# Four heads of scores per chain, values summed per query tile in one PSUM bank, and branch hints moved forward, in a fused attention and expert kernel

## The chip, the cores and the metric

The kernel runs on one core of a Trainium2 chip. The metric is the device time of one execution in microseconds; the number compared is the median of several runs. The engines are TensorE (PE in the profile, its weight loads PEld), VectorE (DVE), ScalarE (ACT), GpSimd (POOL) and SyncE (SP), whose queue issues nearly all transfers.

## The reference, cut to what matters

Three layers run one after the other, all in float32. Only the first is touched by most of the change; the second is where the branches are.

```python
# attention: batch 4, 8 heads, 768 positions, head size 64
scores = scale * np.matmul(q, k.transpose(0, 1, 3, 2))
keep = (pos[None, :] < 4) | ((rel >= 0) & (rel < 128))
scores = np.where(keep, scores, -1e9)
a = softmax(scores)
x = np.matmul(a, v)                      # to 3072 rows of 512
# experts: 8, each 512 -> 1024 -> 512; a row goes to one expert
e_idx = np.argmax(x @ w_gate + modality_bias[modality_id], axis=1)
out[mask] = gate_w[mask, None] * (np.maximum(x[mask] @ w1[e], 0.0) @ w2[e])
# last layer: 512 -> 2048 -> 512 on all rows
h = x @ w_in
out = (h / (1 + np.exp(-1.702 * h))) @ w_out
```

## The kernel before, in words

**Attention** (`attention`, lines 41 to 415) goes through 24 query tiles of 128 rows, six for each of four sequences. A tile sees its own 128 keys, the 128 before them and four sink keys, so a head's scores are 128 x 260 (128 x 128 in the first tile of a sequence). Heads are worked in four couples c, two heads a per couple. For each tile: q and k are transposed (`qtrans`, `ktrans`, lines 152 and 163) and copied out (`qevac`, `kevac`); `scores` (line 182) multiplies one couple, the two heads on the two halves of the array's rows; `mask` (196, VectorE) adds the mask and finds the extreme; `expo` (205, ScalarE) takes the exponential; `ptrans` (217) transposes the probabilities of a couple; `pevac` (240) copies them to SBUF, even couples on ScalarE, odd ones on VectorE; `pv` (270) multiplies by the values; `oevac` (288, ScalarE) copies the sums out; `back` (293) transposes them back and adds the sinks' part; `norm` (313, VectorE) divides and SP stores the rows; `logits`, `then` and `pick` choose the expert of each row. A tile's sinks go through `sinksplit`, `sinktrans` and `sinkevac`.

A float32 product is issued as two passes, and two heads of a couple use halves of the array, so that their passes run side by side. The probabilities lie in `pts` so that one product of a value tile with 256 columns serves two query tiles: those keys as "own" keys of one and as "previous" keys of the next. The sums of two neighbouring query tiles therefore lie side by side in each of two PSUM banks `ops`, one bank per four heads; they are cleared by ScalarE (`zero`, line 266) and every product adds to them.

PSUM has eight banks: three for the small tiles of tag "t" (transposes, `back`; line 55, `NT_BUFS` in 442), two for `ops`, three for scores (line 96, `NS_BUFS` in 441).

The order of all this is written out by numbers: `AT` (line 30) gives each kind of step a due time, in units of one couple (four to a tile), `kinds` (352) says how many couples one call covers, and lines 355 to 415 sort all calls by time and emit them. Each engine then works through its instructions in that order. `OPEN` (37) and `MORE` (38) give the due times of the start of the expert layer, which is mixed into the end of attention: the first expert with 256 rows among the first 16 tiles is found, its weights are loaded and split (`split`, line 1198), its first rows are gathered and transposed (`x0`, `x1`), and its first products (`first0`, `first1`) are issued, while the last tiles are still on their way.

**Experts** (`layers`, line 1103). Rows are handled in pairs of 128-row slots (`pair`, 1407) and then in lone slots (`one`, 1505), an expert's weights in eight chunks f. How many pairs and lone slots there are is known at run time only. So the pairs from the ninth on and all lone slots stand in nested `tc.If`, whose condition is a register loaded from `sx` by `counts` (1444); the body of each is followed in the code by that of the next, and leaving is a branch to the `Else` far behind. Ahead of each such branch stands a hint (`hint`, 1288): a value of 0 or 1 is loaded from rows 7 and 8 of `sx` on all five engines, and a hint instruction with this register says whether the branch will be taken. It stands at chunk f == 6 of the pair or lone slot. Within the lone slots, loads of the next weights stand in an `If` for all engines (1496).

**Last layer**: `up` and `down` over six groups of 512 rows, twice.

Of the kernel before, what the change touches and what calls it, by code (L numbers as in the profile page):

```python
# [21 lines left out]
E = 8  # L22
# [7 lines left out]
AT = dict(sinkevac=13.229, oevac=13.14, qevac=-3.201, kevac=-0.864, scores=-0.497, mask0=0.153, mask1=0.329, expo0=0.53, ptrans=2.608, pevac=3.3,  # L30
          expo1=1.235, pv=6.555, qtrans=-4.329, ktrans=-1.83, back=14.129, sinktrans=12.315, norm=14.975, logits=18.7, then=19.826, pick=23.746,
          guard=7.159, invert=12.135, zero=5.2, sinksplit=8.053)
PVU = 2
# [3 lines left out]
OPEN = dict(split1=2.989, x0=5.244, split0=4.299, x1=5.358, split2=5.494, split3=6.448, first0=6.769, first1=7.711, split4=14.718)  # L37
MORE = 85.058, 0.617, 92.724, 1.445


def attention(tc, cst, late, first, spare, q, k, v, wg, xd, then, pick, at_tile, more, opening):
# [8 lines left out]
    with ExitStack() as ctx:  # L50
# [33 lines left out]
        NV, NG = 6, 3  # L84
        zs = per.tile([P, 1], F32, name="zs")
        nc.gpsimd.memset(zs, 0.0)


        pts = per.tile([P, NG, 4, 2, 2, P], F32, name="pts")
        ops = [ps_o.tile([P, 2, 2, P], F32, name=f"ops{i}") for i in range(2)]  # L90
# [91 lines left out]
        def scores(t, c):  # L182
# [3 lines left out]
            for a in range(2):  # L186
# [26 lines left out]
        def where(t, kk):  # L213

            return kk if t % NG else 1 - kk

        def ptrans(t, c):
            i = t % NT
            ps = ps_t.tile([P, 2, 2, P], F32, name=f"pt{t}_{c}", tag="t")
            k0, k1 = where(t, 0), where(t, 1)  # L220
            for a in range(2):
                h = 2 * c + a
                if i > 0:
                    nc.tensor.transpose(ps[:, k0, a, :], pn[t][:, h, 0:P], ident)
                    nc.tensor.transpose(ps[:, k1, a, :], pn[t][:, h, KB : KB + P], ident)
                else:
                    nc.tensor.transpose(ps[:, k1, a, :], pn[t][:, h, 0:P], ident)
            tps[("p", t, c)] = ps

        def pview(t, c, x):  # L230
            if t % NT == 0:
                return x[:, t % NG, c, :, t % 2, :]
            a, b = sorted(((t - 1) % NG, t % NG))
            return x[:, a : b + 1 : b - a, c, :, t % 2, :]

        def psrc(t, c):
            ps = tps[("p", t, c)]
            return ps[:, where(t, 1)] if t % NT == 0 else ps
# [103 lines left out]
        def fill(n):  # L342
            for _ in range(n):
                nc.tensor.matmul(ops[1].rearrange("p c i t -> p (c i t)")[:, 0:256], cst["nothing"][:, 0:P], cst["nothing"], start=True, stop=True)
# [3 lines left out]
        def ok(t):  # L348
# [3 lines left out]
        kinds = dict(sinkevac=(4, sinkevac), oevac=(2, oevac), qevac=(4, qevac), kevac=(4, kevac), scores=(1, scores), mask0=(1, lambda t, c: mask(t, 2 * c)),  # L352
                     mask1=(1, lambda t, c: mask(t, 2 * c + 1)), expo0=(1, lambda t, c: expo(t, 2 * c)), expo1=(1, lambda t, c: expo(t, 2 * c + 1)),
                     ptrans=(1, ptrans), pevac=(1, pevac), pv=(PVU, pv), qtrans=(4, qtrans), ktrans=(4, ktrans), back=(2, back), sinktrans=(4, sinktrans), norm=(2, norm), logits=(4, logits), then=(4, lambda t: then(t, lgs.pop(t))), pick=(4, pick), guard=(4, guard), invert=(4, invert), zero=(2, zero), sinksplit=(4, sinksplit))
# [3 lines left out]
        for g in range(2):  # L358
            todo.append((len(F2) + .001, zero, (0, g)))
        for nm, (size, fn) in kinds.items():  # L360
            for n in range(0, 4 * T, size):
                t, c = divmod(n, 4)
                if nm in ("qtrans", "qevac", "ktrans", "kevac", "zero") and t == 0 or nm.startswith("sink") and t % NT < 2:
# [1281 lines left out]
```

## Time and profile before

| what | value |
|---|---|
| runs | 1102.95, 1104.8, 1104.44 us; median 1104.44 |
| profiled execution | 1102.95 us, span 1101.4 us from the first to the last instruction |
| TensorE busy | 1068.0 us, 97% of the span, 6625 products |
| VectorE, ScalarE, GpSimd busy | 553.7, 418.2, 241.9 us |
| mean granted TensorE clock | 0.989 of full speed |

The profile is one execution. Times in its rows are microseconds from the start of the span. L194 is line 194 of the kernel before. In timelines, rows of one kind that follow each other are joined (x4), with the start of the first; a note in brackets gives the idle time of the engine just before the row and what ended it. The duration of a product runs to its modelled end; products overlap, so what one costs is read from start to start.

### The profile page before, as it was taken

To read this page: it belongs to the slowest core of one execution; us is meant where nothing else is said; L and a number is where in the kernel's file an instruction comes from. 1 tells how busy PE (TensorE), PEld (TensorE's weight loads), DVE (VectorE), ACT (ScalarE), POOL (GpSimd) and SP (SyncE) were. 2 spreads that over 40 slices of the span, in tenths; PEclk is the share of its full clock that TensorE was granted. 3 is DMA by queue.
4 is the path that set the end of the run, shared out by engine and by line. 5 is a ranking of instruction groups with operands and counts; after the bars stand their busy time and mean duration, and the time that the engine had idled before them with its cause. 6 is when DMAs were issued, how large, how long until landed. Compare 5 with 4: busy or idle time off the path is not lost. (4 is left out here: it accounts for less than half of the span.)

```text
span 1101.4 us, 18806 instructions
## 1 busy us (share of the span) xinstructions
PE 1068.0 (97%) x6625; PEld 904.5 (82%) x6625; DVE 553.7 (50%) x1385; ACT 418.2 (38%) x1026; POOL 241.9 (22%) x397
## 2 busy tenths in 40 slices
PE   6999999978999999999989999999999999999996
PEld 4676767668999999999978888888888888888885
DVE  3767767886555665522114665655623424334232
ACT  3887778742223332222222332332323222222221
POOL 2532231253243342211001213222200101001011
PEclk8999999998999999999999999999999999999998
DMA  6555565451445532216561322302203303124011
GB/s 122 127 125 126 112 138 118 103 146 60 136 123 161 181 98 79 79 52 197 172 217 55 115 83 73 113 8 70 77 1 115 91 24 116 32 83 153 1 39 39
DMA packets 172115, 108.91 MB, mean 99 GB/s; under 512 B 118000, under 2 KB 149744, under 8 KB 171984
## 3 DMA queue, kind: packets, MB, share of 16 engines
q1 hardware_dynamic: 167184, 91.62, 30.1%
q0 software_dynamic: 4800, 15.73, 4.3%
q8 instruction: 60, 0.98, 0.4%
q14 instruction: 71, 0.58, 0.2%
HBM read 79.85 MB, written 27.48 MB: 97 GB/s over the span
## 5 line engine op out<-in xcount | busy, mean ns | idle before, releaser
L1170 PE MATMUL pu<-xh,wah 128*128 128x256 f32 (+1 forms) x576 | 185.6, 322 | 0.0
L1170 PE MATMUL pu<-xh,wal 128*128 128x256 f32 (+1 forms) x576 | 184.2, 320 | 0.4 <-DVEq L1279 0.4
L1555 DVE TENSOR_TENSOR raw<-pu,raw 128x512 f32<-128x512 f32 x96 | 66.3, 691 | 235.2 <-ACT raw L1554 232.7
L1170 PE MATMUL pu<-xl,wah 128*128 128x256 f32 (+1 forms) x576 | 184.2, 320 | 0.1
L1554 ACT ACTIVATE raw<-pu 128x512 f32<-128x512 f32 x96 | 57.5, 598 | 291.9 <-PE pu L1170 291.2
L1185 PE MATMUL pa<-h,wah 128*128 128x256 f32 x768 | 155.4, 286 | 0.0
L1185 PEld LDWEIGHTS pa<-h,wah 128*128 128x128 f32 x768 | 128.0, 194 | 0.0
L1170 PEld LDWEIGHTS pu<-xh,wal 128*128 128x128 f32 x576 | 110.4, 192 | 8.2 <-DVEq L1279 0.6
L1170 PEld LDWEIGHTS pu<-xh,wah 128*128 128x128 f32 x576 | 110.5, 192 | 7.8 <-ACTq L1279 0.2
L1170 PEld LDWEIGHTS pu<-xl,wah 128*128 128x128 f32 x576 | 110.3, 192 | 7.8 <-DVE xl L1123 0.3
L1185 PE MATMUL pa<-h,wal 128*128 128x256 f32 x384 | 109.6, 285 | 0.0
L1193 ACT ACTIVATE h<-pu 128x256 fp32r<-128x256 f32 x96 | 36.8, 383 | 184.2 <-PE pu L1170 182.6
L202 DVE CUSTOM_DVE_ANT_0 sc<-s,m 128x260 f32<-128x260 f32 (+1 forms) x192 | 73.0, 399 | 51.9 <-PE s L194 46.9
L1196 DVE SCALAR_TENSOR_TENSOR h<-pu,h 128x256 fp32r<-128x256 f32 x96 | 40.3, 422 | 110.8 <-ACT h L1193 61.7
L211 ACT ACTIVATE pn<-sc,mx 128x260 f32<-128x260 f32 (+1 forms) x192 | 92.0, 482 | 5.4 <-DVE mx L202 4.7
L1122 ACT ACTIVATE h<-raw 128x512 fp32r<-128x512 f32 x96 | 60.7, 633 | 77.7 <-DVE raw L1555 77.7
L1177 PE MATMUL pa<-wah,h 128*128 128x512 f32 x216 | 76.4, 390 | 0.0
L1177 PE MATMUL pa<-wbh,h 128*128 128x512 f32 x216 | 76.3, 389 | 0.0
L1170 PE MATMUL pu<-xh,wbh 128*128 128x512 f32 x192 | 74.8, 390 | 1.2 <-ACT y L1493 1.2
L1170 PE MATMUL pu<-xh,wbl 128*128 128x512 f32 x192 | 74.7, 389 | 0.0
L1170 PE MATMUL pu<-xl,wbh 128*128 128x512 f32 x192 | 74.7, 389 | 0.0
L1185 PEld LDWEIGHTS pa<-h,wal 128*128 128x128 f32 x384 | 74.6, 194 | 0.0
(327 smaller groups left out, 2055.8 us busy)
## 6 DMA issues: line engine op xcount, KB each, us to landing
raw<-in_moe_w_dram SPq DMA_DIRECT2D x64, 256.0 KB
cd<-yb SPq DMA_DIRECT2D x20, 512.0 KB
xd<-xe SPq DMA_DIRECT2D x24, 256.0 KB
raw<-yp SPq DMA_DIRECT2D x12, 512.0 KB
qn<-in_q_dram SPq DMA_DIRECT2D x22, 256.0 KB
kn<-in_k_dram SPq DMA_DIRECT2D x22, 256.0 KB
vn<-in_v_dram SPq DMA_DIRECT2D x22, 256.0 KB
yb<-y SPq DMA_DIRECT2D x10, 512.0 KB
```

The lines of the kernel that those rows point to most:

```text
L202: nc.vector.tensor_tensor_reduce(out=sc[:, :n], in0=ps[:, :n], in1=m[:, :n], scale=1.0, scalar=3.0e38, op0=ALU.add, op1=ALU.min, accum_out=mx)
L211: nc.scalar.activation(out=pn[t][:, h, :n], in_=sc[:, :n], func=AF.Exp, scale=-1.0, bias=mx, accum_out=sums[t][:, h : h + 1])
L1122: A.activation(out=hi, in_=x, func=AF.Copy)
L1170: nc.tensor.matmul(ps[:, 0:n], w[a][:, s], cols(x, b, k), start=(k == 0 and i == 0), stop=(k == 3 and i == 2))
L1177: nc.tensor.matmul(acc, h[a][:, s], w[b][:, 512:], start=(f == 0 and j == 0), stop=(f == last and j == 2))
L1185: nc.tensor.matmul(acc[:, i % 2 * 256 : i % 2 * 256 + 256], wa[f][a][:, s], h[b], start=(f == 0 and i % 2 == 0 and j == 0), stop=(f == CH ...
L1193: A.activation(out=hi, in_=ps, func=AF.Relu)
L1196: V.scalar_tensor_tensor(out=lo, in0=ps, scalar=0.0, in1=hi.bitcast(F32), op0=ALU.max, op1=ALU.subtract)
L1554: A.activation(out=s, in_=ps, func=AF.Sigmoid, scale=1.702)
L1555: V.tensor_tensor(out=s, in0=ps, in1=s, op=ALU.mult)
```

## The change

In attention, `scores` takes two couples per call (four heads, four banks), `ops` is one bank with 128 columns per couple, `pv` sums a query tile's own and previous keys by itself with 128-column products, so that clearing (`zero`) and the arrangement of `pts` by three key tiles go, and nearly all due times are new. In the expert layer a hint is static ("LikelyTaken") and stands in an `If` that holds only when the exit will be taken; it stands at f == 3 (5 in the last unconditional pair) and, for lone slots, f == 2. Rows 7 and 8 of `sx` go. The `If` around the loads of lone slots runs on SP alone.

```diff
-AT = dict(sinkevac=13.229, oevac=13.14, qevac=-3.201, kevac=-0.864, scores=-0.497, mask0=0.153, mask1=0.329, expo0=0.53, ptrans=2.608, pevac=3.3,
-          expo1=1.235, pv=6.555, qtrans=-4.329, ktrans=-1.83, back=14.129, sinktrans=12.315, norm=14.975, logits=18.7, then=19.826, pick=23.746,
-          guard=7.159, invert=12.135, zero=5.2, sinksplit=8.053)
-PVU = 2
+AT = dict(sinkevac=10.229, oevac=10.224, qevac=-2.123, kevac=-1.366, scores=-0.449, mask0=-0.2, mask1=0.21, expo0=0.692, ptrans=2.608, pevac=3.437,
+          expo1=0.867, pv=7.004, qtrans=-4.358, ktrans=-1.915, back=10.991, sinktrans=9.575, norm=11.395, logits=15.779, then=16.626, pick=20.835,
+          guard=5.52, invert=11.081, sinksplit=8.614)
...
-OPEN = dict(split1=2.989, x0=5.244, split0=4.299, x1=5.358, split2=5.494, split3=6.448, first0=6.769, first1=7.711, split4=14.718)
-MORE = 85.058, 0.617, 92.724, 1.445
+OPEN = dict(split1=4.183, x0=5.146, split0=3.966, x1=5.358, split2=5.428, split3=6.826, first0=6.763, first1=6.923, split4=14.582)
+MORE = 84.738, 0.617, 92.724, 1.62
...
-        pts = per.tile([P, NG, 4, 2, 2, P], F32, name="pts")
-        ops = [ps_o.tile([P, 2, 2, P], F32, name=f"ops{i}") for i in range(2)]
+        ops = ps_o.tile([P, 4, P], F32, name="ops")
+        pts = {}
...
-        def scores(t, c):
+        def scores(t, g):
...
-            for a in range(2):
+            for c, a in ((2 * g, 0), (2 * g, 1), (2 * g + 1, 0), (2 * g + 1, 1)):
...
         def pevac(t, c):
+            if c == 0:
+                pts[t] = p2.tile([P, 4, 2, 2, P], F32, name=f"pts{t}", tag="pts")
+            k = slice(1, 2) if t % NT == 0 else slice(0, 2)
+            x, ps = pts[t][:, c, k], tps.pop(("p", t, c))[:, k]
             if c % 2:
-                nc.vector.tensor_copy(pview(t, c, pts), psrc(t, c))
+                nc.vector.tensor_copy(x, ps)
             else:
-                nc.scalar.activation(out=pview(t, c, pts), in_=psrc(t, c), func=AF.Copy)
+                nc.scalar.activation(out=x, in_=ps, func=AF.Copy)
...
-        def zero(t, g):
-
-            nc.scalar.activation(out=ops[g][:, :, t % 2, :], in_=zs.unsqueeze(2).broadcast_to([P, 2, P]), func=AF.Copy)
-
-        def pv(t, g=None):
+        def pv(t, g):
 
             i = t % NT
-            if i == 0:
-                return
-            kw = dict(start=False, stop=False, skip_group_check=True)
-            for j in [t - 1] + ([t] if i == NT - 1 else []):
-                for h in range(H) if g is None else range(4 * g, 4 * g + 4):
-
-                    c, a = divmod(h, 2)
-                    o = ops[c // 2][64 * a : 64 * a + 64, c % 2]
-                    if j == t - 1:
-                        nc.tensor.matmul(o.rearrange("p i t -> p (i t)"), nat[j]["v"][:, h], pts[:, j % NG, c, a].rearrange("p i t -> p (i t)"), **kw)
-                    else:
-                        nc.tensor.matmul(o[:, t % 2, :], nat[j]["v"][:, h], pts[:, j % NG, c, a, t % 2, :], **kw)
+            for c in (2 * g, 2 * g + 1):
+                for kk in range(i == 0, 2):
+                    for a in range(2):
+                        nc.tensor.matmul(ops[64 * a : 64 * a + 64, c], nat[t - 1 + kk]["v"][:, 2 * c + a], pts[t][:, c, kk, a], start=(kk == 0 or i == 0), stop=(kk == 1), skip_group_check=True)
...
-            nc.scalar.activation(out=ohl[t][:, 2 * g : 2 * g + 2], in_=ops[g][:, :, t % 2, :], func=AF.Copy)
+            nc.scalar.activation(out=ohl[t][:, 2 * g : 2 * g + 2], in_=ops[:, 2 * g : 2 * g + 2], func=AF.Copy)
...
-NS_BUFS = 3
+NS_BUFS = 4
...
-    def hint(label, row, i):
-
-        v = nc.values_load(sx[0:1, row, i : i + 1], engines=ENGINES, min_val=0, max_val=1)
-        tc.mark_branch_hint_location(label, v, engines=ENGINES)
+    def hint(label, n, i):
+
+        with tc.If(n <= i):
+            tc.mark_branch_hint_location(label, "LikelyTaken", engines=ENGINES)
...
-            if f == 5 and u == NP0 - 1:
+            if f == 3 and u == NP0 - 1:
                 counts()
-            if f == 6 and NP0 - 1 <= u < NP - 1:
-                hint(f"pairs{u + 1}", 7, u + 1)
+            if f == (5 if u == NP0 - 1 else 3) and NP0 - 1 <= u < NP - 1:
+                hint(f"pairs{u + 1}", pairs[0], u + 1)
...
         alone.append(nc.values_load(sx[0:1, 2, E + 1 : E + 2], min_val=0, max_val=E))
+        alone.append(flag(2, E + 1, (ET.SP,)))
...
-            with tc.If(alone[0] > s + 1):
+            with tc.If(alone[1] > s + 1):
...
-            if f == 6 and s + 1 < E:
-                hint(f"alone{s + 1}", 8, s + 1)
+            if f == 2 and s + 1 < E:
+                hint(f"alone{s + 1}", alone[0], s + 1)
```

## Rows read from the trace of the kernel before

**Rows 1.** Table by stage: stretch, length, busy time (instructions) by engine, PE clock, DMA share, GB/s.
```profile
67.80:119.50 51.70, 51.70 (x390) 35.35 (x388) 35.43 (x152) 41.32 (x143) 13.24 (x45) 1.00 0.57 123
...
213.00:240.80 27.80, 20.70 (x180) 17.03 (x179) 21.60 (x53) 16.38 (x36) 16.30 (x22) 1.00 0.64 184
```

**Rows 2.** Timeline of PE around a change of sequence: start, duration, what, count.
```profile
110.48 0.71 PE L194 MATMUL s<-kts,qt 64*128 64x260 f32 x4
111.12 1.08 PE L282 MATMUL ops<-pts,vn 128*64 128x256 f32 x8
112.13 0.33 PE L224 MATMUL pt<-ident,pn 128*128 128x128 f32 x1
112.30 0.27 PE L225 MATMUL pt<-ident,pn 128*128 128x128 f32 x1
112.41 0.27 PE L224 MATMUL pt<-ident,pn 128*128 128x128 f32 x1
112.52 0.27 PE L225 MATMUL pt<-ident,pn 128*128 128x128 f32 x1
112.72 0.49 PE L194 MATMUL s<-kts,qt 64*128 64x128 f32 x4
113.14 0.33 PE L224 MATMUL pt<-ident,pn 128*128 128x128 f32 x1
...
113.53 0.27 PE L225 MATMUL pt<-ident,pn 128*128 128x128 f32 x1
...
119.37 1.08 PE L282 MATMUL ops<-pts,vn 128*64 128x256 f32 x8
120.28 0.61 PE L284 MATMUL ops<-pts,vn 128*64 128x128 f32 x8
120.82 0.44 PE L227 MATMUL pt<-ident,pn 128*128 128x128 f32 x2
```

**Rows 3.** Timeline of DVE: the copy of the transposes that ended at 113.53.
```profile
113.84 0.69 DVE L242 COPY pts<-pt 128x512 f32<-128x512 f32 x1 [0.19 <-PE pt L225]
```

**Rows 4.** Timeline of PE on the way out of attention.
```profile
226.12 0.98 PE L1134 MATMUL pu<-ident,xg 128*128 128x128 f32 x7 [1.63 <-ACT xg L1143]
...
233.14 0.37 PE L298 MATMUL bt<-svb,stt 96*128 96x288 f32 x1 [1.47 <-DVE xe L319]
```

**Rows 5.** Timeline of DVE on the way out of attention.
```profile
232.56 0.44 DVE L319 TENSOR_TENSOR xe<-bt,rs 128x288 f32<-128x288 f32 x1
...
234.92 2.35 DVE L675 CUSTOM_DVE_ANT_0 pk_d<-lg,bias 128x8 f32<-128x8 f32 x1 [0.29 <-POOL lg L330]
...
237.88 1.99 DVE L678 SCALAR_TENSOR_TENSOR pk_eq<-pk_d,pk_mx,c_rank 128x8 f32<-128x8 f32 x1
```

**Rows 6.** Groups by line from 20 to 220 us: busy, mean ns, idle before.
```profile
L268 ACT ACTIVATE ops<-zs 128x256 f32<-128x256 f32 x47 | 18.1, 386 | 1.4
```

**Rows 7.** Timeline of POOL on the way out of attention.
```profile
234.85 2.41 POOL L1123 TENSOR_TENSOR wal<-raw,wah 128x1024 fp32r<-128x1024 f32 x1
```

**Rows 8.** Timeline of PE where the lone experts are left.
```profile
563.12 2.02 PE L1491 MATMUL pa<-ca,raw 128*128 128x128 f32 x16 [1.69 <-SPq L1496]
566.37 0.47 PE L1170 MATMUL pu<-xh,wbh 128*128 128x512 f32 x1 [1.23 <-ACT y L1493]
```

**Rows 9.** Hints and branches of PE's queue: ns least/median/most, first and last start.
```profile
L1641 PEldq BRANCH_PREFETCH_HINT x1: 35/35/35, 557.9 to 557.9; - x1
L1528 PEldq COMPARE_BRANCH x1: 3003/3003/3003, 560.0 to 560.0; - x1
L1496 PEldq COMPARE_BRANCH x3: 223/500/2503, 559.3 to 563.7; - x3
L1641 PEldq BRANCH_PREFETCH_HINT x1: 55/55/55, 1.0 to 1.0; - x1
L1072 PEldq COMPARE_BRANCH x1: 494/494/494, 6.8 to 6.8; - x1
```

**Rows 10.** Waits from 526 to 534 us: total, times, longest.
```profile
PE pu L1482 <- DVEq L1384: 0.8, 1, 0.8
```

More of the change, by code (lines that the diff above doesn't have):

```diff
@@ L83, in attention @@
         m0, m1, m2 = cst["m0"], cst["m1"], cst["m2"]
-        NV, NG = 6, 3
-        zs = per.tile([P, 1], F32, name="zs")
-        nc.gpsimd.memset(zs, 0.0)
-        pts = per.tile([P, NG, 4, 2, 2, P], F32, name="pts")
-        ops = [ps_o.tile([P, 2, 2, P], F32, name=f"ops{i}") for i in range(2)]
+        NV = 6
+        ops = ps_o.tile([P, 4, P], F32, name="ops")
+        pts = {}
         sctx = ctx.enter_context(ExitStack())
@@ L211, in expo @@
             nc.scalar.activation(out=pn[t][:, h, :n], in_=sc[:, :n], func=AF.Exp, scale=-1.0, bias=mx, accum_out=sums[t][:, h : h + 1])
-        def where(t, kk):
-            return kk if t % NG else 1 - kk
         def ptrans(t, c):
@@ L219, in ptrans @@
             ps = ps_t.tile([P, 2, 2, P], F32, name=f"pt{t}_{c}", tag="t")
-            k0, k1 = where(t, 0), where(t, 1)
             for a in range(2):
@@ L223, in ptrans @@
                 if i > 0:
-                    nc.tensor.transpose(ps[:, k0, a, :], pn[t][:, h, 0:P], ident)
-                    nc.tensor.transpose(ps[:, k1, a, :], pn[t][:, h, KB : KB + P], ident)
+                    nc.tensor.transpose(ps[:, 0, a, :], pn[t][:, h, 0:P], ident)
+                    nc.tensor.transpose(ps[:, 1, a, :], pn[t][:, h, KB : KB + P], ident)
                 else:
-                    nc.tensor.transpose(ps[:, k1, a, :], pn[t][:, h, 0:P], ident)
+                    nc.tensor.transpose(ps[:, 1, a, :], pn[t][:, h, 0:P], ident)
             tps[("p", t, c)] = ps
[L230 to L238, printed above, removed]
         def pevac(t, c):
+            if c == 0:
+                pts[t] = p2.tile([P, 4, 2, 2, P], F32, name=f"pts{t}", tag="pts")
+            k = slice(1, 2) if t % NT == 0 else slice(0, 2)
+            x, ps = pts[t][:, c, k], tps.pop(("p", t, c))[:, k]
             if c % 2:
-                nc.vector.tensor_copy(pview(t, c, pts), psrc(t, c))
+                nc.vector.tensor_copy(x, ps)
             else:
-                nc.scalar.activation(out=pview(t, c, pts), in_=psrc(t, c), func=AF.Copy)
+                nc.scalar.activation(out=x, in_=ps, func=AF.Copy)
         stt, sts = {}, {}
@@ L343, in fill @@
             for _ in range(n):
-                nc.tensor.matmul(ops[1].rearrange("p c i t -> p (c i t)")[:, 0:256], cst["nothing"][:, 0:P], cst["nothing"], start=True, stop=True)
+                nc.tensor.matmul(ops.rearrange("p c t -> p (c t)")[:, 0:256], cst["nothing"][:, 0:P], cst["nothing"], start=True, stop=True)
         fill(F1)
@@ L349, in ok @@
             return 0 <= t < T
-        kinds = dict(sinkevac=(4, sinkevac), oevac=(2, oevac), qevac=(4, qevac), kevac=(4, kevac), scores=(1, scores), mask0=(1, lambda t, c: mask(t, 2 * c)),
+        kinds = dict(sinkevac=(4, sinkevac), oevac=(2, oevac), qevac=(4, qevac), kevac=(4, kevac), scores=(2, scores), mask0=(1, lambda t, c: mask(t, 2 * c)),
                      mask1=(1, lambda t, c: mask(t, 2 * c + 1)), expo0=(1, lambda t, c: expo(t, 2 * c)), expo1=(1, lambda t, c: expo(t, 2 * c + 1)),
-                     ptrans=(1, ptrans), pevac=(1, pevac), pv=(PVU, pv), qtrans=(4, qtrans), ktrans=(4, ktrans), back=(2, back), sinktrans=(4, sinktrans), norm=(2, norm), logits=(4, logits), then=(4, lambda t: then(t, lgs.pop(t))), pick=(4, pick), guard=(4, guard), invert=(4, invert), zero=(2, zero), sinksplit=(4, sinksplit))
+                     ptrans=(1, ptrans), pevac=(1, pevac), pv=(2, pv), qtrans=(4, qtrans), ktrans=(4, ktrans), back=(2, back), sinktrans=(4, sinktrans), norm=(2, norm), logits=(4, logits), then=(4, lambda t: then(t, lgs.pop(t))), pick=(4, pick), guard=(4, guard), invert=(4, invert), sinksplit=(4, sinksplit))
         todo = []
@@ L357, in attention @@
             todo.append((n + AT["scores"] + .001, fill, (some,)))
-        for g in range(2):
-            todo.append((len(F2) + .001, zero, (0, g)))
         for nm, (size, fn) in kinds.items():
@@ L362, in attention @@
                 t, c = divmod(n, 4)
-                if nm in ("qtrans", "qevac", "ktrans", "kevac", "zero") and t == 0 or nm.startswith("sink") and t % NT < 2:
+                if nm in ("qtrans", "qevac", "ktrans", "kevac") and t == 0 or nm.startswith("sink") and t % NT < 2:
                     continue
@@ L410, in attention @@
         todo.append((last("scores", "mask0", "mask1"), close, (sctx, "scores")))
-        todo.append((last("pv", "zero", "expo0", "expo1"), close, (tctx, "values")))
+        todo.append((last("pv", "expo0", "expo1"), close, (tctx, "values")))
         for nm, time in OPEN.items():
@@ L952, in steps @@
     def steps():
-        sx = pool.tile([P, 9, NQ], I32, name="sx")
+        sx = pool.tile([P, 7, NQ], I32, name="sx")
         V.memset(sx, 0)
@@ L981, in steps @@
             V.tensor_tensor(out=sx[:, r], in0=y, in1=new, op=ALU.mult)
-            if r == 1:
-                V.tensor_copy(sx[:, 7], y)
-        V.tensor_scalar(out=sx[:, 8, 0:E], in0=cst["col"][:, 0:E], scalar1=e1[:, E : E + 1], scalar2=None, op0=ALU.is_lt)
         V.tensor_scalar(out=sx[:, 2, E : E + 1], in0=e2[:, E : E + 1], scalar1=0.5 / P, scalar2=1.0, op0=ALU.mult, op1=ALU.add)
```

## Prediction

> **What bounds the kernel now.** I read the table by stage first. In the attention stage TensorE is busy in 51.70 of 51.70 us at full clock, with ScalarE at 41.32 and VectorE at 35.43 [rows 1]. A busy share alone does not show that TensorE sets the pace, so the second view is its timeline there: chain follows chain with the same lengths every time, 0.64 us for two heads of scores, 1.01 us for four heads of values [rows 2]. An engine that waited for others would show varying gaps. So a tile costs what its chains cost, and the reader is to see that a chain costs more than its columns: something is paid whenever the kind of work changes. The third view is the way from attention into the experts, 213 to 240.8 us, where TensorE is busy for 20.70 of 27.80 us [rows 1], and the fourth the leaving of the lone experts, where it stands still twice (below). The steps between (pairs of experts, 267.6 to 533.5 us) and the last layer run without a gap, and no edit touches their work.
>
> **Scores and values, the prices.** All from [rows 2], start to start. Inside a run of transposes one takes 0.11 (112.41 to 112.52). The first after values takes 0.17 (112.13 to 112.30), the last before scores 0.20 (112.52 to 112.72): such a run pays 0.06 + 0.09 = 0.15 for being entered and left. A chain of two heads of scores takes 0.64 with 260 keys (110.48 to 111.12) and 0.42 with 128 (112.72 to 113.14). It has four passes in two side-by-side pairs, so 2 x 132 columns cost 0.22, 2 x 260 columns 0.43, and the remaining 0.21 is paid per chain. Eight passes of values with 256 columns take 1.01 (111.12 to 112.13); eight with 256 and eight with 128 take 1.45 (119.37 to 120.82). So eight with 128 cost 0.44, eight with 256 twice that, and a chain of values pays about 0.15 on top.
>
> **What the change makes of it.** Per tile there are two chains of scores for four, two runs of transposes and the like for four, and still two chains of values, which now hold 16 passes of 128 columns for 8 of 256: 0.88 + 0.15 = 1.03 for 1.01. That is 2 x 0.21 + 2 x 0.15 - 2 x 0.02 = 0.68 us less per tile. The first tile of each of the four sequences has no values today and gets two chains: 0.30 of overhead, so it saves 0.38 (its own columns, 2 x 0.44, are those that the last tile of the sequence gives up). 20 x 0.68 + 4 x 0.38 = **15.1 us less**.
>
> **What it adds there.** The three small PSUM banks are taken in turn by transposes, q or k, transposes, and then `back`, which now stands last in the run and needs the bank of the first transposes. Its copy by VectorE is over 1.00 us after the last of these began (113.53 to 113.84 + 0.69) [rows 2, 3]; TensorE has 9 x 0.11 = 0.99 us to do until `back`. TensorE went on 0.14 us after a VectorE operation that freed a bank had ended (232.56 + 0.44 to 233.14) [rows 4, 5]. So `back` is about 0.15 late, in two runs of each of 20 tiles (those of first tiles copy half as much): 40 x 0.15 = **6.0 us more**. Behind the waiting `back` stand values and scores, so all of it counts. Ends: 0 if another bank is free, 0.35 each (14 us) if VectorE is one more row late.
>
> **What costs nothing while its cover holds.** The cleared accumulators go: 47 ScalarE activations, 18.1 us [rows 6], on an engine that was not the limit. Four score banks for three: the next chain needs its first bank half a tile later, some 4 us, and VectorE has 35.43 / 12 = 3.0 us of work in each half of the six tiles of that stage [rows 1]. If that cover goes, each half tile stretches by what is missing. The probabilities keep two buffers of a tile, read long before the next but one. SP issues the same loads in the same order; the first expert's weights come later in its order by up to 1.2 of the planner's steps, behind the stores of tile rows that come earlier, and the first use of the late ones is after routing begins. The loads of hint values from memory go on five engines; a compare on each comes in their place, in stretches where TensorE runs without gaps and its sequencer is ahead.
>
> **The way out of attention.** In the new order `back` of tile 22 is ahead of the first expert's transposes and that of tile 23 behind all else. The 1.47 us stop before it, for a VectorE operation that stood behind other work [rows 4], goes: **1.5 less**, or nothing if ScalarE's copy of the values is late instead. The 1.63 us stop for the gathered rows [rows 4] stays, as the value chains between lookup and use are as many. After the last `back`, two VectorE operations of 8 columns took 2.35 and 1.99 us [rows 5], the first for the length of a GpSimd split that began just before it (234.85, 2.41 us) [rows 7]. The last choice of experts is ordered ahead of one split now: I take half of one, **1.2 less**, between 0 and 4.3.
>
> **The hints.** On TensorE the hint for leaving the lone experts ran at 557.9, the branch at 560.0 took 3.00 us, and TensorE stood still for 1.69 us [rows 8, 9]. A jump without any hint, at 563.7, took 2.50 [rows 9]: 2.1 us of notice bought nothing. With notice of 5.8 us (1.0 to 6.8), at the start of the program, a branch over a long body took 0.49 [rows 9]. The change moves the hint from the seventh to the third of eight chunks; a chunk is two groups of eight passes of 0.11 us, so that is 7 us more. I side with the long notice: **1.7 less**, between 0 and 2.9, as the second stop of 1.23 [rows 8] follows the unhinted jump. At the exit of the pairs TensorE waited 0.8 us for VectorE [rows 10], which had the last sums to copy, not for code: nothing there. The Trainium skill, "Runtime: NRT & Kernel Launch", section "Instruction fetch mechanics", says that fetching ahead is purely sequential and that a taken branch to code outside the window forces a fetch before anything goes on. By that the hint would buy nothing at any distance; the first two rows agree, the third does not.
>
> **The sum.** -15.1 + 6.0 - 1.5 - 1.2 - 1.7 = -13.5 us. The profiled execution took 1102.95 (span 1101.4), so 1089.4; the median of the runs shown is 1.5 above it, so **1090.9** for the median. What a measurement of this kernel can tell from no change is about 0.2%, 2.2 us.
>
> **Rivals.**
> *Hints do nothing.* For it: 3.00 us with a hint, 2.50 without. Against: 0.49. It gives 1092.6.
> *The waits for banks are at their upper end.* For it: `back` has no slack in the new order. Against: VectorE is idle for three tenths of the stage [rows 1], so it is seldom a row late. 14 for 6: 1099.
> *Slower: the one accumulator bank is a gate.* Today each group of four heads has its bank, with two halves, and a copy-out has most of a tile of time. After the change each chain of values must wait for ScalarE's copy-out of the same heads of the tile before, twice per tile. If ScalarE gets to it late by x, TensorE stands for x in each of 48 chains; from 13.5 / 48 = 0.28 us on, the change loses, and at 0.45 the time is 1112. Against: the copy is as large as a clearing, under 0.4 [rows 6], there are some 3 us between two chains of values, and ScalarE, busy for 0.8 of the stage [rows 1], loses the 18.1 us of clearing. [...]
> *The new value passes don't run side by side.* Then 16 passes cost 16 x 0.11 and a chain 0.88 more: 1130. Against: eight passes of 128 columns take 0.44 today in the same alternation of halves.
>
> **How the numbers follow.** Forecast with working hints 0.57, with idle ones 0.24, upper bank waits 0.08, gate 0.06, no pairing 0.02, no change by other causes 0.03. The first three are faster but for 0.02 of the bank case that could end near zero: faster 0.88, same 0.05, slower 0.07. Low end: no bank waits (-6.0) and some of the 3.1 us of split and the 1.2 us of the second stop, 1082. High end: half of the added bank waits and idle hints, with the small terms gone, 1098.
>
> **What would show it.** Right: four-head chains of scores of 1.07 us, chains of values of 1.03, two of each per tile; a tile 0.5 us shorter; no L268 rows; idle time before `back` put down to VectorE's or ScalarE's copies; the lone experts' exit branch under 0.5 us and no stop before the first L1491 row behind it. Wrong: chains of values that begin late after ScalarE's copy-out; gaps inside a chain of scores; a tile as long as today; a stop at the exit as long as today.

## The result, and the profile after

| | before | after |
|---|---|---|
| median of four runs each | 1104.62 us | 1093.67 us (1092.24 to 1094.46) |
| ratio, 95% interval | | 0.9899, 0.988 to 0.9918 |
| profiled execution, span | 1102.95, 1101.4 us | 1093.89, 1092.3 us |
| TensorE busy, products | 1068.0 us, 6625 | 1059.9 us, 6945 |
| ScalarE busy | 418.2 us | 406.1 us |

The change is 11 us faster. The forecast was 1090.9 within 1082 to 1098: direction and range hold, and the time came out 2.8 us above the forecast by the median and 4.5 us above it in the profiled execution (1093.89 against 1089.4). Line numbers below are those of each kernel; L191 after is L194 before, and so on.

The table by stage, the stretch that answers to the first of [rows 1] and the way out of attention (stretch, length, busy time by engine in the order PE, PEld, DVE, ACT, POOL, PE clock, DMA share, GB/s):

```profile
66.67:116.45 49.78, 49.64 (x470) 39.80 (x470) 35.27 (x152) 38.59 (x130) 13.19 (x45) 1.00 0.58 129
205.30:233.70 28.40, 22.05 (x213) 18.48 (x210) 22.05 (x55) 16.08 (x36) 17.35 (x25) 1.00 0.63 180
```

Six tiles take some 1.9 us less in these windows, 0.32 a tile, 80 more products included. ScalarE's 41.32 has become 38.59, but TensorE, still without a real gap, sets the pace. The way out of attention is no shorter.

The timeline of PE in the new order, one half tile, which answers to [rows 2]:

```profile
92.40 1.15 PE L191 MATMUL s<-kts,qt 64*128 64x260 f32 x8
93.47 0.33 PE L216 MATMUL pt<-ident,pn 128*128 128x128 f32 x1
...
93.86 0.27 PE L217 MATMUL pt<-ident,pn 128*128 128x128 f32 x1
93.97 0.60 PE L153 MATMUL qp<-ident,qn 128*128 128x128 f32 x4
...
94.73 0.27 PE L217 MATMUL pt<-ident,pn 128*128 128x128 f32 x1
95.01 0.73 PE L275 MATMUL bt<-btw,oh 128*128 128x144 f32 x4
95.67 1.09 PE L258 MATMUL ops<-pts,vn 128*64 128x128 f32 x16
96.69 1.15 PE L191 MATMUL s<-kts,qt 64*128 64x260 f32 x8
```

The timeline of DVE, the copy that `back` waits for, which answers to [rows 3], and that of ACT, the copies of the summed values out of their bank:

```profile
94.17 0.69 DVE L228 COPY pts<-pt 128x512 f32<-128x512 f32 x1
```

```profile
92.55 0.36 ACT L265 ACTIVATE oh<-ops 128x256 f32<-128x256 f32 x1
...
97.00 0.38 ACT L265 ACTIVATE oh<-ops 128x256 f32<-128x256 f32 x1
```

Four heads of scores take 1.07 (92.40 to 93.47), a chain of values 1.02 (95.67 to 96.69). The last transpose before `back` is followed after 0.28 us and not 0.11: the copy of the first transposes ends at 94.86, `back` starts 0.15 later, at 95.01.

The timeline of PE on the way out, which answers to [rows 4], with the first product of routing:

```profile
218.63 0.33 PE L1102 MATMUL pu<-ident,xg 128*128 128x128 f32 x1
220.38 0.98 PE L1102 MATMUL pu<-ident,xg 128*128 128x128 f32 x7 [1.42 <-ACT xg L1111]
...
225.06 0.29 PE L272 MATMUL bt<-svb,stt 96*128 96x288 f32 x1
...
233.74 0.24 PE L797 MATMUL pt<-pk_oh,c_ones 128*128 128x192 bf16 x1 [4.14 <-DVE pk_oh L644]
```

The timelines of DVE and of POOL there, which answer to [rows 5] and [rows 7]:

```profile
224.24 0.42 DVE L1164 SCALAR_TENSOR_TENSOR h<-pu,h 128x256 fp32r<-128x256 f32 x1 [1.00 <-ACT h L1161]
...
227.09 0.46 DVE L293 TENSOR_TENSOR xe<-bt,rs 128x288 f32<-128x288 f32 x1
227.47 2.18 DVE L647 CUSTOM_DVE_ANT_0 pk_d<-lg,bias 128x8 f32<-128x8 f32 x1
...
229.58 2.39 DVE L650 SCALAR_TENSOR_TENSOR pk_eq<-pk_d,pk_mx,c_rank 128x8 f32<-128x8 f32 x1
231.89 0.45 DVE L293 TENSOR_TENSOR xe<-bt,rs 128x288 f32<-128x288 f32 x1
...
232.67 0.17 DVE L647 CUSTOM_DVE_ANT_0 pk_d<-lg,bias 128x8 f32<-128x8 f32 x1
```

```profile
223.07 2.41 POOL L1091 TENSOR_TENSOR wal<-raw,wah 128x1024 fp32r<-128x1024 f32 x1 [3.27 <-ACT wah L1090]
...
227.22 4.73 POOL L1091 TENSOR_TENSOR wal<-raw,wah 128x1024 fp32r<-128x1024 f32 x2
```

The stop before the `back` of tile 23 is gone, that for the gathered rows is there. Two operations of 8 columns are stretched again, 2.18 and 2.39 us, and the second ends with the second of the two GpSimd splits (229.58 + 2.39 = 231.97, 227.22 + 4.73 = 231.95); the same operation as the first takes 0.17 once the splits are over.

The timeline of PE where the lone experts are left, which answers to [rows 8], and the hints and branches of PE's queue (least, median, most, in ns), which answer to [rows 9]:

```profile
553.61 2.84 PE L1460 MATMUL pa<-ca,raw 128*128 128x128 f32 x24
557.39 0.47 PE L1138 MATMUL pu<-xh,wbh 128*128 128x512 f32 x1 [0.94 <-ACT y L1462]
```

```profile
L1610 PEldq BRANCH_PREFETCH_HINT  x2: 40/42/45, 509.5 to 542.9; - x2
L1497 PEldq COMPARE_BRANCH  x2: 358/1170/1982, 552.5 to 554.3; - x2
```

The hint for the lone exit runs at 542.9, 9.6 us ahead of the exit branch at 552.5, which takes 0.36 us where it took 3.00 before; the first stop is gone. The jump behind it at 554.3, which has no hint, takes 1.98, and the stop of TensorE after it is still there.

### The profile page after: what moved, and what is told of

The parts are those of the page before. It is cut to its first block, busy times and chain, and to the rows that moved or that the text cites. A ratio compares the mean times of both kernels' runs of the same rounds, so it can differ in the third digit from the quotient of the medians.

```text
span 1092.3 us, 19270 instructions
## 1 busy us (share of the span) xinstructions
PE 1059.9 (97%) x6945; PEld 920.8 (84%) x6945; DVE 552.9 (51%) x1383; ACT 406.1 (37%) x978; POOL 241.5 (22%) x396
## 4 chain that ended last, share of the span: by engine, by line
PE 47%; issue 4%; POOL 0%; ACT 0%; POOLq 0%; DVE 0%; ACTq 0%
PE pu L1138 22%; PE pa L1145 17%; PE pu L1145 6%; PE pu L1451 1%; PE pa L1460 1%; POOL out_dram L1548 0%; POOLq L1610 0%; DVE raw L1524 0%; PE pt L1102 0%; ACT xs L1121 0%; ACT raw L1523 0%; ACT y L1462 0%; ACT ca L1453 0%; POOLq L1548 0%; ACTq L1462 0%
```

## The experiments

"From the first scores" below is the span of the profiled execution less the start of the first scores, which came at 15.5 to 17.6 us in the fourteen profiles, whatever the kernel. It is 1084.4 before and 1075.7 after. "The lone stretch" is from the first product of the lone experts to the first of the last layer: 32.84 before, 30.59 after.

### The hints without the new order

The new hints in the kernel before, with all that comes with them: their places, the counts read earlier, the `If` on SP alone, and rows 7 and 8 of `sx` gone. Attention stays as it was.

```diff
...
-            if f == 6 and s + 1 < E:
-                hint(f"alone{s + 1}", 8, s + 1)
+            if f == 2 and s + 1 < E:
+                hint(f"alone{s + 1}", alone[0], s + 1)
...
```

> The kernel before with the new hints alone; attention is that of before. My theory: early static hints are worth the stop at the exit of the lone experts and part of the one behind it, 1.7 to 2.3 us of 1104, so 1102.4; on TensorE the exit branch takes under 0.5 us (3.00 before), no stop before the first L1491 row behind it, and the pairs' exit keeps its 1.12 us gap. Rival 'hints do nothing, the traces differ by chance': branch 2.5 to 3 us, time 1104.5. Rival 'the loads of hint values on five engines cost time too': more than 2.5 us less, and a shorter stretch from the first unconditional pair to the last pair.

Measured: 1100.98 beside 1104.16, ratio 0.9967 (0.9957 to 0.9978). The stop in the middle of the lone exit is gone and the lone stretch takes 30.43 us. The exit branch, the jump behind it, and TensorE's first product of the last layer:

```profile
L1526 PEldq COMPARE_BRANCH  x2: 192/762/1332, 558.9 to 560.7; - x2
```

```profile
563.62 0.47 PE L1167 MATMUL pu<-xh,wbh 128*128 128x512 f32 x1 [0.78 <-issue]
```

The branch itself took 1.33, not under 0.5: the time came out better than expected, the duration of the branch worse. The jump took 0.19 here, and TensorE still stood for 0.78, so the second stop is for the most part not the jump's. The rival that hints do nothing falls. The sign of the third one, that the loads of hint values cost time too, did come: more than 2.5 us less. But `early_register` below keeps these loads and gains as much, and from routing's first product to the lone experts it is as long as before (292.71 for 292.70).

### The new order without the hints

The changed kernel with the hints of before (the edit above, reversed).

> The changed kernel with the hints of before (register, chunk 6). My theory: the two halves add up, so 1093.7 + 2.2 = 1095.9, 0.992 of before; attention, tail and routing as in the changed kernel (routing at full rate by 261.7 us, 268.4 before); the exit branch of the lone experts is at 3 us again and the stop of 1.7 is back. Rival 'the hints were worth nothing and the exit got shorter because of where the code lies now': 1093.7, exit branch under 0.5 us.

Measured: 1095.28, ratio 0.9918 (0.9903 to 0.9934). The lone stretch is 31.45, the exit branch (least, median, most, in ns):

```profile
L1499 PEldq COMPARE_BRANCH  x1: 2121/2121/2121, 553.2 to 553.2; - x1
```

Routing was where the changed kernel has it (its first product at 233.77). The ratios multiply to 0.9918 x 0.9967 = 0.9885, which lies within the interval of the whole. So the order brings about 9 us and the hints the rest: by the medians 3.2 us in the old order, and in the new one 1.6 beside the first median of the changed kernel (1093.67) and 1.0 beside its second (1094.33, below), which is hard to tell from none.

### Notice or form of the hint

The kernel before with its register hints moved forward, and the changed kernel with its static hints moved back:

```diff
...
-            if f == 6 and s + 1 < E:
+            if f == 2 and s + 1 < E:
                 hint(f"alone{s + 1}", 8, s + 1)
```

> The kernel before with its register hints at the new, earlier chunks (3 and 5 for pairs, 2 for lone slots). Theory 'notice is what counts': exit branch of the lone experts under 0.5 us, 1.7 to 2.3 us less than before. Rival 'the static form is what counts': branch 2.5 to 3 us, time as before, 0.998 to 1.002.

Measured: 1101.13, ratio 0.9973 (0.9963 to 0.9983), 3 us less than before; the lone stretch is 30.62.

```diff
...
-            if f == 2 and s + 1 < E:
+            if f == 6 and s + 1 < E:
                 hint(f"alone{s + 1}", alone[0], s + 1)
```

> The changed kernel with its static hints at the old place, chunk 6. Theory 'notice is what counts': the exit branch of the lone experts takes 2 to 3 us with some 2 us of notice, the stop behind it is back, 1.7 to 2.3 us more than the changed kernel: 1095.9. Rival 'the static form is what counts': branch under 0.5 us, 1093.7.

Measured: 1094.41, ratio 0.991 (0.9892 to 0.9928); the lone stretch is 31.54. The rows of the exit branch, first with the early register (the most of three branches is the exit), then with the late static hint (the exit and the jump behind it):

```profile
L1528 PEldq COMPARE_BRANCH  x3: 65/65/456, 531.8 to 560.4; - x3
```

```profile
L1497 PEldq COMPARE_BRANCH  x2: 2109/2673/3237, 551.3 to 553.7; - x2
```

With a register 10 us ahead the branch takes 0.46. With the static form 1.6 us ahead it takes 2.11, and the jump behind it 3.24. **Notice counts, the form does not**, by the duration of the branch and the lone stretch. The price is smaller than expected in the new order: the time is 0.7 above the first median of the changed kernel and 0.1 above its second, too little to tell from none, and the lone stretch is 0.95 longer. All eleven profiles with the early place (most of them below) have a lone stretch of 30.4 to 30.7, the three with the late one 31.4 to 32.8.

### Two heads per chain of scores again

```diff
-kinds = dict(... scores=(2, scores) ...
+kinds = dict(... scores=(1, scores) ...
...
-        def scores(t, g):
+        def scores(t, c):
...
-            for c, a in ((2 * g, 0), (2 * g, 1), (2 * g + 1, 0), (2 * g + 1, 1)):
+            for a in range(2):
```

> The changed kernel with scores of one couple per call again, so two heads per chain; due times, the four score banks and the summing of values are those of the changed kernel, and by the due times every second chain of scores falls between the two runs of transposes. My theory, prices per chain and per run: 48 chains more, each 0.21 of its own and 0.15 for the run that it cuts, 17.3 us; it gives 0.64 us of other work between the transposes and the back-transposition, so the wait of 6.9 us goes; 1093.7 + 17.3 - 6.9 = 1104, a tile 0.4 us longer. Rival 'the gain is from the values and the clearing, not from the chains of scores': 1092 to 1096.

Measured: 1101.03, ratio 0.9974 (0.9963 to 0.9986), 7.4 us above the changed kernel, 8.6 from the first scores. The timeline of PE:

```profile
93.16 0.27 PE L217 MATMUL pt<-ident,pn 128*128 128x128 f32 x1
93.26 0.66 PE L275 MATMUL bt<-btw,oh 128*128 128x144 f32 x4
93.85 1.09 PE L258 MATMUL ops<-pts,vn 128*64 128x128 f32 x16
94.87 0.71 PE L191 MATMUL s<-kts,qt 64*128 64x260 f32 x4
95.51 0.33 PE L216 MATMUL pt<-ident,pn 128*128 128x128 f32 x1
```

`back` follows the transposes after 0.10: the wait is gone, as expected, 0.7 us in all for 6.9. Put back, 48 chains cost (8.6 + 6.2) / 48 = 0.31 each, where 0.36 was expected. The rival that the gain is from the values and the clearing, 1092 to 1096, falls. With 1101.03 this kernel, which has the new hints, the new value chains, the new due times and no clearing, is where the kernel before with the new hints alone is (1100.98). So the four-head chains carry the gain of the order, and what else the order brings, the 18.1 us less of ScalarE's clearing included, comes to nothing on balance. No run takes these other parts one by one.

### `back` behind the values

```diff
-AT = dict(... back=10.991, ...
+AT = dict(... back=11.04, ...
```

> The changed kernel with one due time moved: back 10.991 to 11.04, so that it follows the chain of values instead of the transposes. Theory 'the 0.15 before it is a wait for the bank, until VectorE's copy ends': the wait goes, and two more changes of the kind of work come instead, by the rows 0.20 + 0.31 + 0.22 for 0.11 + 0.15 + 0.22 + 0.20 per half tile; 0.05 x 45 = 2 us more, 1093.7 to 1097, and the first product of back starts at the same distance each time. Rival 'it is the price of going from transposes to back': then 0.2 x 45 = 9 us more, 1103.

Measured: 1094.82, ratio 0.9912 (0.9896 to 0.9929), from the first scores 1075.9. The timeline of PE:

```profile
95.33 0.27 PE L217 MATMUL pt<-ident,pn 128*128 128x128 f32 x1
95.53 1.09 PE L258 MATMUL ops<-pts,vn 128*64 128x128 f32 x16
96.55 0.76 PE L275 MATMUL bt<-btw,oh 128*128 128x144 f32 x4
97.24 1.15 PE L191 MATMUL s<-kts,qt 64*128 64x260 f32 x8
```

The rival is out: 1103 was its price. No such wait is left, and a half tile (92.99 to 97.24) takes 4.25 against 4.29, six tiles 49.75 against 49.77, so the new changes of work cost what the wait had. `two_chains` too has `back` straight behind the transposes and does not wait, so it is a real wait and not the price of going from the one to the other; with this order of work it is not worth moving.

### The way out of attention

```diff
-OPEN = dict(... split2=5.428, ...
+OPEN = dict(... split2=5.05, ...
```

> The changed kernel with the third weight split due before the transposes of the gathered rows instead of behind them (split2 5.428 to 5.05). ScalarE can do its half in the 1.4 us in which it waits for these rows, and GpSimd then starts its row of splits some 3 us sooner. My theory, VectorE's operations of 8 columns are held until GpSimd's split ends: one of the two blocked ones (2.18 and 2.39 us) goes, the product behind the last choice starts at 231.5 (233.74 in the changed kernel), 1091.5. Rival 'the tail goes by something else, a blocked operation is cover only': 1093.7, product at 233.5 or later.

Measured: 1093.32, ratio 0.9903 (0.9887 to 0.992): no gain. My theory's arrangement missed its aim: the first split did start sooner, but ScalarE's halves of the next two still waited for the first expert's products, GpSimd was splitting at 229.52 and 232.19, and two operations were held for 2.05 and 1.75 us. That tells nothing of the theory.

```diff
-OPEN = dict(split1=4.183, x0=5.146, split0=3.966, x1=5.358, split2=5.428, split3=6.826, first0=6.763, first1=6.923, split4=14.582)
+OPEN = dict(split1=4.183, x0=16.9, split0=3.966, x1=16.905, split2=16.91, split3=16.93, first0=16.92, first1=16.94, split4=16.95)
```

> The changed kernel with the first expert's transposes, its third to fifth weight splits and its first products due behind the last choice of experts (x0 16.9, x1 16.905, split2 16.91, first0 16.92, split3 16.93, first1 16.94, split4 16.95), so the last tile's back-transpositions are ahead of them on TensorE and no split runs on GpSimd beside the last choice. My theory, the way from the last tile to routing sets the time and the blocked operations cost 4 us of it: no operation of 8 columns over 0.4 us, the choice done by 223, TensorE busy with the first expert until some 228 and the routing's first product then, 5 us sooner; 1088 to 1090. Rival 'the splits and copies moved behind the choice collide with the routing on VectorE and GpSimd': routing as much later as it began sooner, 1092 to 1095.

Measured: 1092.13, ratio 0.9892 (0.9876 to 0.9909), just inside the rival's range; from the first scores it is 2.5 less, half of the gain that my theory expected, and operations were held all the same. The choice was done at 224.4, 9 us sooner, but routing's first product had to stand behind the first expert's (230.63), and the splits now met the routing. The timelines of DVE and POOL:

```profile
230.15 1.70 DVE L772 TENSOR_TENSOR pk_d<-pk_d,pk_mx 128x64 f32<-128x64 f32 x1
...
232.36 1.80 DVE L821 TENSOR_TENSOR r_n<-r_cx 128x8 f32<-128x8 f32 x1
...
234.59 2.08 DVE L777 TENSOR_SCALAR g_sm<-g_sm 128x8 f32<-128x8 f32 x1
```

```profile
229.37 4.76 POOL L1091 TENSOR_TENSOR wal<-raw,wah 128x1024 fp32r<-128x1024 f32 x2 [1.70 <-ACT wah L1090]
...
234.25 2.40 POOL L1091 TENSOR_TENSOR wal<-raw,wah 128x1024 fp32r<-128x1024 f32 x1
```

Each ends with a GpSimd split, and two more of 2.08 (234.59) and 1.65 (237.58) follow, beside the splits from 234.25 and 236.83. These two work on one tile and a constant, so the hold here doesn't need two tiles read from SBUF, the on-chip memory. The stretched operations go where the splits go; that is what the next kernel takes away.

```diff
-OPEN = dict(... split4=14.582)
+OPEN = dict(... split4=16.9)
...
-SPLIT_V = (0, 1, 3)
+SPLIT_V = range(8)
```

> The changed kernel with every weight split of the first expert on VectorE (SPLIT_V all eight) and the fifth one due behind the last choice (split4 16.9). No GpSimd split is left beside the last choice and the routing. Theory 'VectorE's small operations are held until GpSimd's split ends': no operation of 8 columns over 0.4 us in the tail, the routing's first product at 229.5 us against 233.74 after the same start, TensorE not stopped there and so not at half clock behind it; in the routing the 4.7 us of two more blocked operations pay for the splits that VectorE takes over (1.25 us each): 1088 to 1090. Rival 'the long times come from VectorE itself or from memory traffic': the small operations stay long, VectorE has 5 us more work, 1094 to 1099.

Measured: 1091.04, ratio 0.9887 (0.9871 to 0.9904), from the first scores 3.4 less. The timeline of DVE at the last choice:

```profile
227.58 0.16 DVE L647 CUSTOM_DVE_ANT_0 pk_d<-lg,bias 128x8 f32<-128x8 f32 x1
...
227.66 0.22 DVE L650 SCALAR_TENSOR_TENSOR pk_eq<-pk_d,pk_mx,c_rank 128x8 f32<-128x8 f32 x1
```

The operations that took 2.18 and 2.39 take 0.16 and 0.22. Routing's first product comes at 229.69, with a start of the scores 0.6 later, and TensorE is at full clock there, where it was at 0.50 from 234.2 to 237.6 after its long stop. The rival falls. The gain is 1 us short of the expectation, and the trace has a longer stop further on, 4.39 us where the changed kernel has 2.58, for an operation of GpSimd that follows VectorE's part of the routing:

```profile
244.51 0.32 PE L912 MATMUL pa<-r_bt,r_at 128*128 128x29 f16 x6 [4.39 <-POOL r_bt L905]
```

```diff
-OPEN = dict(split1=4.183, x0=5.146, split0=3.966, x1=5.358, split2=5.428, split3=6.826, first0=6.763, first1=6.923, split4=14.582)
+OPEN = dict(split1=4.183, x0=16.9, split0=3.966, x1=16.905, split2=16.91)
...
-SPLIT_V = (0, 1, 3)
+SPLIT_V = range(8)
...
-ADV = [(0, 7), (4, 8), (5, 1), (12, 0), (12, 2), (11, 5)]
+ADV = [(3, 3), (3, 3), (4, 2), (6, 2), (4, 0), (12, 2), (11, 5), (0, 0)]
...
-    for f in range(2, CH):
-        first(0, f, xt[0], 2 * P, lambda: advance(ADV[f - 2][0]))
-        down_pair(0, f - 2)
+    advance(7)
+    for f in range(CH):
+        first(0, f, xt[0], 2 * P, lambda: advance(ADV[f][0]))
+        if f > 1:
+            down_pair(0, f - 2)
         if f + 3 < CH:
             split(f + 3)
-        advance(ADV[f - 2][1])
+        advance(ADV[f][1])
```

> As the last one, and the order of the tail turned round: the first expert's transposes and third split due behind the last choice (x0 16.9, x1 16.905, split2 16.91), and its first two chunks of products taken behind the start of the routing instead of into the end of attention, with seven steps of the routing ahead of them. Theory 'the way from the last tile through the routing to the second pair sets the time, and TensorE's work of the first expert can be its cover': the choice done by 224, the routing's first product by 225, the gathers of the second pair some 8 us sooner than in the changed kernel; 1084 to 1088. Rival 'VectorE, with the splits, becomes the bound of this stretch': the first product early, but pairs of experts begin no sooner than with the splits alone, 1088 to 1091.

Measured: 1090.49, ratio 0.9883 (0.9867 to 0.99), 0.4 less from the first scores than the last one. Routing's first product is at 224.06, 9.7 us sooner than in the changed kernel, yet little of that is gained, and the time lies in the rival's range. That it is VectorE that bounds the stretch, as the rival says, this run does not show; `route_first2` speaks against it.

The changed kernel once more, beside the last version:

> The changed kernel itself once more, beside the next one, so that the two stand against the same runs. Whatever the theory: 0.990 of before, TensorE's idle time and half-clock stretches of the tail as in its first profile; only the start of the first scores differs from execution to execution (15.5 to 17.6 us in the profiles so far).

Measured: 1094.33, ratio 0.9898 (0.9877 to 0.992), from the first scores 1077.1. This profile has a longer stop for the gathered rows (2.46 for 1.75 from one product to the next) and 7.8 us from the `back` of tile 23 to routing's first product, where the first profile had 8.7 and the kernel before 7.7.

The last version, against `route_first`:

```diff
-OPEN = dict(split1=4.183, x0=16.9, split0=3.966, x1=16.905, split2=16.91)
+OPEN = dict(split1=5.42, x0=16.9, split0=5.41, x1=16.905, split2=16.91)
...
-ADV = [(3, 3), (3, 3), (4, 2), (6, 2), (4, 0), (12, 2), (11, 5), (0, 0)]
+ADV = [(4, 4), (4, 4), (5, 3), (6, 0), (12, 2), (11, 5), (0, 0), (0, 0)]
...
-        if f + 3 < CH:
-            split(f + 3)
+        if f in (0, 1, 3, 4, 5):
+            split(f + (3 if f < 2 else 2))
```

> The routing ahead of the first expert, with all splits on VectorE, and two more moves: the first two splits behind the normalizing of tile 22 (they held it back by 2.6 us), the routing's gathered products one chunk earlier and one split fewer ahead of them. Theory 'VectorE is now the bound of this stretch, until the last four 4.7 us operations of the routing': routing's first product 1 us and the gathered products 2 us sooner than in the last kernel, 1088 to 1090. Rival 'TensorE's own work is the bound behind the routing': as the last kernel, 1090.5.

Measured: 1089.97, ratio 0.9862 (0.9841 to 0.9882). The gathered products come 3 us sooner (238.50 for 241.53), the time from the first scores is 0.3 less. The time alone does not decide between the theory (1088 to 1090) and the rival (1090.5); the trace speaks for the rival, that TensorE's own work behind the routing is the bound: it is busy for 17.49 of the 19.50 us from 238.5 to 258, at a mean granted clock of 0.82. No run tests this. **This version beats both kernels**: its slowest run, 1090.52, is 2.5 us below the fastest of the changed kernel beside it, 1093.06.

## Why the prediction was right, and where its size was off

The terms, by the two profiled executions (start to start on TensorE):

| step | predicted | measured |
|---|---|---|
| fewer changes of work in attention | -15.1 | -14.5 |
| `back` waits for its bank | +6.0 | +6.9 |
| stop before the `back` of tile 23 | -1.5 | -1.5 |
| last choice beside the splits | -1.2 | +1.0 |
| hints | -1.7 | -2.2 |
| new waits for VectorE, tiles 20 to 23 | none | +1.2 |
| first scores start sooner, rest | none | 0.0 |
| sum | -13.5 | -9.1 |

All are differences of one profile each. The first two rows come from adding up TensorE's starts by kind of work, from the first scores to the `back` of tile 23 (216.18 us before, 208.45 after): scores 59.84 and 48.84, transposes of probabilities 46.65 and 39.11, of q and k 22.12 and 21.08, values 44.17 and 45.67, `back` 29.42 and 35.47, sinks' transposes 4.79 and 2.03, other work 9.20 and 9.37, waits for a bank 0 and 6.88. A change of work is counted with the kind that it leaves, so only the sum of the kinds can be held against the prediction: 14.8 less without waits for a bank and other work, 1.5 of it the stop that went; the rest is 13.3, and 14.5 if the new waits of 1.2 us are told apart. Of these 14.5 some 0.4 is not a change of work: it is a wait for VectorE that only the kernel before has, at 196.03.

**The prices per chain** held: 1.07 and 1.02 us were measured where 1.07 and 1.03 were worked out, and the wait for the bank was 0.18 in 39 places for 0.15 in 40. `two_chains` and `back_behind` show that both are what they were called. The sign "a tile 0.5 us shorter" did not follow from the prediction's own terms, (15.1 - 6.0) / 24 = 0.38; the middle tiles gave 0.32.

**The rival of the one accumulator bank** fell. ScalarE's copy-outs lie between the chains of values (92.55 and 97.00, with a chain from 95.67 to 96.69), and no chain starts late for one. The Trainium skill, "PSUM — Partial Sum Buffer", section "PSUM bank collisions raise a hardware error", asks to guard a bank against two engines by its quadrants of 32 partitions, or more simply as a whole, and not by address; chains and copy-outs here cover all partitions, and the trace has them alternate. No run here shows what happens otherwise.

**The step that failed** is "the last choice of experts is ordered ahead of one split now: I take half of one, 1.2 less, between 0 and 4.3". Neither of the two held operations went. They took 2.35 + 1.99 us in the kernel before, 2.18 + 2.39 in the changed one and 2.40 + 1.88 in its second profile: the choice of tile 22 still stands between the two normalizings of tile 23, with two splits in a row beside it. From the first `back` product of tile 23 to routing's first product it is 8.7 us and 7.8 in the second profile, where it was 7.7: 1.0 more in the one, 0.1 in the other, and nothing less in either. The holds make up 0.2 of the 1.0. In the same profile the first normalizing of tile 23 began 2.0 us after that `back` product (225.06 to 227.09), with a split of VectorE's own ahead of it, where it began 0.9 us after it in the kernel before (233.14 to 234.04). What the rest of the 1.0 is due to, no run tests. The sign was taken from the order of the due times, although ScalarE's half of a split and not its due time sets when GpSimd begins, as `split_first` shows. The range given did not reach to a loss.

That a split holds VectorE at all, which the prediction read off one pair of rows, is now shown by `all_vector`. The Trainium skill, "SBUF — State Buffer", section "Who interferes with whom", states that a VectorE instruction with two SBUF inputs contends with a GpSimd one that reads SBUF, over ports that it calls an exclusive lock. The trace agrees: the operation on SBUF ended at 231.97, with the split at 231.95, while the operation on products in PSUM at 224.24 took 0.42 in the middle of a split (223.07 to 225.48).

**The term that was missing** is a wait for VectorE in tile 20: its `reciprocal` for the gates (L778, 1.75 us at 187.44) delays the masks, and the transposes at 190.90 start 0.84 us late; 0.31 more follows at 199.88:

```profile
187.44 1.75 DVE L778 RECIPROCAL g_sl<-g_sm 128x256 f32<-128x256 f32 x1
```

```profile
190.90 0.33 PE L216 MATMUL pt<-ident,pn 128*128 128x128 f32 x1 [0.68 <-DVE pts L228]
```

The prediction looked for cover in the middle tiles alone, where no such work runs.

**The hints** were taken with the right reason and 0.5 us too small in the traces. The Trainium skill, "Runtime: NRT & Kernel Launch", section "Instruction fetch mechanics", has fetching ahead as purely sequential, by which no such gain should come; the measured 0.36 and 0.46 us with some 10 us of notice (1.33 in `hints_alone`, without a stop of TensorE), against 2.1 to 3.0 with about 2, decide against that for a hinted branch. One bound of the prediction stands: the pairs' exit kept its stop (1.125 us from one product to the next, 1.122 before). The other has the wrong reason: the second stop does stay, but for the most part not because of the unhinted jump. With a jump of 0.19 us TensorE stood for 0.78 (`hints_alone`), with one of 1.98 for 0.94, and with the 2.50 of before for 1.23.

Why the exit branch took 3.00 before and 2.1 with nearly the same notice in two other kernels stays open, as does why the hints are worth 3.2 us on the old order and about 1 on the new one. The traces narrow the second question: behind the late-hinted branch TensorE stood for 1.69 us in the kernel before, for 0.44 in `order_alone` and without a stop that the profile shows in `late_static`, whose next stop is 1.52. There is one trace of each.

## What to carry to other kernels

Where TensorE runs without gaps, count its changes from one kind of work to another and price them from start to start. Taking work off another engine, as the clearing here, need gain nothing by itself: look at what it does to TensorE's chains. Hint a branch far ahead: ten microseconds served here and two did not, in either form. In a dependent tail, keep long GpSimd passes over SBUF away from VectorE's small operations on SBUF; it was cheaper here to give VectorE the whole work.

## What the runs showed that was not expected

- The five splits of GpSimd, moved to VectorE, shorten the way, though VectorE is the engine waited for: a split takes it 1.22 us, and beside one of GpSimd's (2.4 us) a 0.17 us operation takes up to 2.39.
- The half clock moves with the stops. In the changed kernel TensorE's granted clock was 0.50, its 1.2 GHz level, from 234.2 to 237.6 after the stop of 4.14 us; in `all_vector`, without this stop, the same work ran at 1.00, but it was at 0.50 from 245 to 251 after the stop of 4.39 us. From 225 to 265 us the mean is 0.87 in both, so this clock is no part of the gain of `all_vector`. In the second profile of the changed kernel the work behind a stop of 3.27 us ran at 1.00 (234 to 238). The two tables, changed kernel and `all_vector`:

```profile
225.00:265.00 40.00, 31.27 (x242) 30.12 (x242) 29.80 (x78) 10.78 (x21) 17.93 (x14) 0.87 0.27 75
```

```profile
225.00:265.00 40.00, 33.60 (x269) 32.52 (x269) 28.57 (x100) 12.76 (x24) 6.50 (x8) 0.87 0.29 80
```
